# A chunked linear-attention and squared-ReLU kernel: how w and u are spread, how U and Y of the first chunks are interleaved, and a new order of the opening

## The chip, the core and the metric

The kernel runs on one core of a Trainium2 chip. The core has a matrix engine (TensorE, "PE" in the profile; its weight loads are "PEld"), a vector engine (VectorE, "DVE"), a scalar engine (ScalarE, "ACT"), a general engine (GpSimd, "POOL") and a queue engine (SyncE, "SP"). Each runs its own instructions in order and waits for the others by semaphores. Matrix products write to PSUM, eight banks of 128 x 512 fp32; everything else lies in SBUF, 128 partitions. The metric is device time in microseconds, the median of several runs; smaller is better.

## The reference

For each batch b (4) and head h (8), with 768 time steps and head size 48, a state of 48 x 48 is carried along:

```python
for t in range(S):
    cur = u[:, :, None] * k_t * v_t          # outer product over (d, e)
    y[:, :, t] = r_t @ (state + cur)
    state = w[..., None] * state + k_t * v_t
```

Here `w` and `u` have one value for each head and position, 8 x 48. The outputs of all heads form x, 3072 x 384, and the second half is a feed-forward layer: `(max(x @ w_in, 0) ** 2) @ w_out` with 2048 hidden columns, the result in fp32.

## The kernel before

**Tiling.** Time is cut into 24 units of 128 steps: six chunks for each of four batches. In a unit, all heads lie beside each other. The recurrence is done in closed form in a unit: k is multiplied by a decay factor `Wk` (rows w to a power that depends on the step) and r by `Wt`; both are transposed; their products give 128 x 128 scores for each head, masked by a triangle (`Bm`); Y is the scores times v plus r times the carried state `S0W`; U is k times v, which updates the state, scaled by `WLm`. The diagonal term is `dv` = v times the row sum of r x k x u (steps `P0`, `P1`, `du`, `dv`).

**Pairs.** The first four units (`PAIRED = 4`) are two pairs, two chunks of one batch each, loaded by one transfer per tensor (`lp`): partition p holds steps 2p and 2p + 1 of the 256. So the first chunk of a pair lies on partitions 0 to 63 and the second on 64 to 127. Half a in the names below is the even or odd step, half x (or s) the chunk. Products for a chunk of a pair therefore work on 64 rows of TensorE: U of a pair's chunk is eight products of 64 rows (L463), Y is two products with the identity that put dv in place (L428), four with the state for a second chunk (L436) and sixteen with the masked scores (L440).

**Factors.** `w` (L257) brings w as one row. `lw` (L266) takes its logarithm, `bw` (L269) multiplies a column of ones with that row and so spreads it over 128 partitions in a bank, and four Exp steps with a scale for each partition (L294, L298) make the factors of the pairs. `bc` (L303) puts the logarithm into columns, from which `WLcol` and `WLm` (L314) come. `u` is spread in the same way (`bu`, L272) and copied to SBUF (`ub`). `tab` loads ScalarE's tables ahead of that.

**Feed-forward.** `X` transposes a unit's outputs on TensorE (L489), `xTc` copies them; `xX` does both by a transposing transfer. `F1` (L505) multiplies with w_in, `re` and `sq` are ReLU and square, `F2` (L533) and `Fh` (L547) multiply with w_out; `os` and `out` copy and store. w_in comes in four pieces (`V`, L331) and w_out in four (`W`, L334) by transfers that GpSimd issues; SP issues the loads of r, k and v (`lp`, L325, `ld`, L321). `Z` (L565) multiplies the identity with itself into a bank that nobody reads: an empty product.

**Order.** The order of everything is written out by hand in `ORDER`. A step reads `name.unit...:engine/slots`, where the engine is A (ScalarE), D (VectorE), G (GpSimd), P (TensorE) or S (SP), and the slots say which bank or buffer the result takes. Each engine runs its own steps in this order. `Z.8:P/0` is two products of 512 columns, `Z.2` two of 128, `Z.7` one of 512 and three of 128. A `T` step transposes k and r of one unit past the pairs (L398), `TK` and `TR` those of a pair (L364), `KC` and `RC` copy them out of the bank, `Ap` and `Bp` are a pair's scores and masks (L384, L392).

Of the kernel before, what the change touches and what calls it, by code (L numbers as in the profile page):

```python
# [32 lines left out]
P1.3:G Bp.1.0.1:D/4 F1.0.0:P/6 re.0.3:D/0 dv.2:G F1.1.3:P/5 Wt.2:A re.0.0:A/1 W.1:G Bp.1.1.1:D/5 du.3:D/3 ld.v.5:S/5  # L33
Bp.1.0.0:D/6 Wk.2:A F1.1.0:P/4 F1.1.1:P/6 dv.3:G re.1.0:A/2 F1.0.1:P/0 rh.5:G/4 re.1.3:A/3 Bp.1.1.0:D/7 Y.3:P/4
sq.1.3:A/0 re.0.1:A/4 W.2:G kh.4:D/5 re.1.1:A/5 sq.1.0:D/1 Y.2:P/5 ld.k.6:S/6 xs.3:D/2 W.3:G F1.0.2:P/0 xs.2:A/3
rh.4:D/5 sq.0.0:A/2 X.3:P/6 W.0:G X.2:P/4 re.0.2:D/3 F1.1.2:P/5 xTc.3:A/0 sq.0.3:A/3 xTc.2:D/0 re.1.2:A/2 P0.4:D/4
T.4:P/0 Tc.4:D/4 F1.2.4:P/6 F1.2.7:P/4 sq.1.2:D/4 F1.2.5:P/5 re.2.4:D/1 re.2.7:A/0 ld.r.6:S/6 sq.0.2:A/5 F1.2.1:P/0
re.2.5:D/2 re.2.1:A/3 sq.2.5:D/6 sq.0.1:D/7 F1.2.0:P/6 kh.5:D/4 F1.2.2:P/4 sq.2.1:A/8 F1.2.6:P/5 re.2.2:A/2 re.2.0:D/4
T.5:P/0 re.2.6:D/3 F2.0.2:P/4 F1.2.3:P/6 ld.r.7:S/7 Tc.5:A/5 P1.4:D du.4:D/4 sq.1.1:D/9 A.4:P/5/0 sq.2.6:A/10
re.2.3:A/5 sq.2.3:A/11 F2.0.1:P/4 sq.2.0:A/12 F2.0.3:P/4 vb.4:G/4 Bm.4.1:D/0 Bm.4.0:D/1 sq.2.7:A/13 P0.5:D/1 A.5:P/6/0  # L40
Bm.5.1:D/2 sq.2.4:A/14 F2.1.1:P/5 Bm.5.0:D/3 F2.1.2:P/5 ld.k.7:S/7 dv.4:G Y.4:P/0 P1.5:G du.5:D/0 F2.3.2:P/6
sq.2.2:A/15 ld.v.7:S/6 ld.k.9:S/0 xs.4:D/4 F2.0.0:P/4 vb.5:A/5 Y.5:P/0 dv.5:D xs.5:D/0 F2.3.0:P/6 P0.6:G/0 P1.6:G
ld.v.6:S/7 F2.3.1:P/6 os.0:D/0 ld.r.9:S/0 X.4:P/0 xTc.4:D/1 U.4:P/4 F2.1.0:P/5 X.5:P/0 F2.1.3:P/5 S0.4:D xTc.5:D/1
rh.7:G/6 F1.3.0:P/4 os.1:D/1 F1.3.4:P/0 P0.7:G/2 re.3.0:D/3 out.1:S F1.3.2:P/5 kh.7:D/6 re.3.4:A/5 kh.6:G/0 F1.3.6:P/4
# [24 lines left out]
re.6.6:D/2 dv.13:G F2.9.0:P/0 XB.14:S/0 sq.6.6:A/15 du.12:D/3 A.13:P/2/1 sq.6.5:A/8 A.12:P/5/7 re.6.1:D/5 F2.8.1:P/4
sq.6.7:A/12 XB.15:S/6 Bm.12.0:D/2 P0.17:G/1 sq.6.2:A/16 F2.8.3:P/4 Bm.12.1:D/3 re.6.3:A/4 F2.8.0:P/4 ld.v.14:S/7  # L70
# [54 lines left out]
def kernel(  # L125
# [106 lines left out]
    for t in rk:  # L232
        nc.vector.memset(t[:, :, :, D:DP], 0.0)
# [403 lines left out]
```

## Time and profile before

| | us |
|---|---|
| median of three runs | 170.84 (170.64 to 170.85) |
| profiled execution, whole time | 171.19 |
| its span, first to last instruction | 169.5 |
| TensorE busy | 164.2 |
| VectorE busy | 137.1 |
| ScalarE busy | 101.9 |
| GpSimd busy | 99.9 |

The times below are microseconds from the start of the span. A group line names the line of the kernel, the engine, the operation, what it writes and reads, and how many there are. An engine's busy time counts matrix products as pipelined, so that products that overlap are one stretch; the end of a matrix product is modelled.

### The profile page before, as it was taken

The page shows a single profiled execution, that of the slowest core. Times are in us where ns is not written, and L with a number is a line of the kernel's source. Part 1 is how long each engine was busy: PE and PEld are TensorE (multiplying, and loading weights), DVE is VectorE, ACT ScalarE, POOL GpSimd, SP SyncE. Part 2 cuts the span into 40 slices and gives each one's busy share as a digit, 9 for nine tenths or more (in the row PEclk, how much of TensorE's full clock was granted, in tenths as well). Part 3 has the DMA queues.
Part 4 walks back from the last instruction along what each step waited for, and adds up shares of the span by engine and source line. Part 5 has one row for each costly group of instructions (what it writes and reads, how often), then busy time and mean ns, then how long its engine had stood idle before and what let it go on. Part 6 is the DMA issues. An engine that isn't in the chain of part 4 may idle for free.

```text
span 169.5 us, 4602 instructions
## 1 busy us (share of the span) xinstructions
PE 164.2 (97%) x1828; PEld 125.4 (74%) x1828; DVE 137.1 (81%) x255; ACT 101.9 (60%) x190; POOL 99.9 (59%) x122
## 2 busy tenths in 40 slices
PE   4999999999999999999999999999999999999993
PEld 1686989767866786888766888766888676898762
DVE  5669989997899999979999999998779975955300
ACT  4684686870685779249892359952099393254731
POOL 6799681277199608996699979399627550200000
PEclk9999999999999999999999999999999999999999
DMA  5999999991899798999997999965959672230032
GB/s 136 323 237 193 215 215 208 201 200 39 165 200 211 138 191 173 209 201 134 209 203 151 212 228 220 177 136 141 184 98 202 170 88 70 90 99 0 6 139 93
DMA packets 96137, 27.56 MB, mean 163 GB/s; under 512 B 90642, under 2 KB 96020, under 8 KB 96116
## 3 DMA queue, kind: packets, MB, share of 16 engines
q1 hardware_dynamic: 92416, 22.55, 66.4%
q0 software_dynamic: 2816, 3.54, 11.5%
q10 hardware_dynamic: 884, 1.18, 2.2%
q8 instruction: 14, 0.23, 0.6%
q14 instruction: 7, 0.06, 0.1%
HBM read 20.45 MB, written 4.72 MB: 149 GB/s over the span
## 4 chain that ended last, share of the span: by engine, by line
PE 95%; ACT 1%; DVE 1%; issue 1%; ACTq 0%
PE bank L505 37%; PE bank L533 36%; PE bank L411 3%; PE bank L463 2%; PE bank L452 2%; PE bank L364 2%; PE bank L489 2%; PE bank L450 2%; PE bank L547 2%; PE bank L440 1%; PE bank L269 1%; DVE Bm L392 1%; PE bank L303 1%; PE bank L272 1%; PE bank L398 1%; PE bank L428 1%
## 5 line engine op out<-in xcount | busy, mean ns | idle before, releaser
L505 PE MATMUL bank<-xT,W 128*128 128x256 bf16 (+1 forms) x672 | 70.0, 257 | 0.0
L533 PE MATMUL bank<-W,hq 128*128 128x384 bf16 x368 | 68.9, 326 | 0.0
L505 PEld LDWEIGHTS <-W 128*128 128x128 bf16 x672 | 56.9, 98 | 7.7
L515 ACT ACTIVATE hr<-bank 128x512 bf16<-128x512 f32 x67 | 38.7, 594 | 36.4 <-PE bank L505 27.8
L533 PEld LDWEIGHTS <-hq 128*128 128x128 bf16 x368 | 33.8, 98 | 18.2
L522 ACT ACTIVATE hq<-hr 128x512 bf16<-128x512 bf16 x70 | 41.0, 626 | 3.4 <-DVE hr L517 2.8
L419 DVE TENSOR_TENSOR Bm<-bank,maskJT 128x512 bf16<-128x512 f32 x40 | 25.7, 682 | 2.7 <-PE bank L411 2.7
L355 POOL TENSOR_TENSOR dv<-ldv,du 128x384 f32<-128x384 f32 (+1 forms) x18 | 15.9, 891 | 16.2 <-DVE du L350 11.3
L517 DVE TENSOR_SCALAR hr<-bank 128x512 bf16<-128x512 f32 x29 | 19.7, 686 | 6.6 <-PE bank L505 4.5
L347 POOL TENSOR_TENSOR P<-P,ub 128x384 f32<-128x384 f32 x15 | 16.0, 1070 | 13.1 <-DVE P L343 12.7
L340 POOL TENSOR_TENSOR rk<-ldr,Wt 128x384 bf16<-128x384 f32 x15 | 16.4, 1101 | 0.0
L343 POOL TENSOR_TENSOR P<-ldr,ldk 128x384 f32<-128x384 f32 x13 | 13.3, 1023 | 1.5 <-DMA ldk<-in_k_dram 1.2
L524 DVE TENSOR_TENSOR hq<-hr 128x512 bf16<-128x512 bf16 x26 | 12.4, 490 | 2.0 <-ACT hr L515 1.8
L484 POOL TENSOR_TENSOR S0W<-ts,WLm 128x384 bf16<-128x384 f32 x10 | 10.9, 1091 | 4.4 <-DVE ts L481 3.6
L475 DVE TENSOR_TENSOR xs<-bank,dv 128x384 bf16<-128x384 f32 x20 | 11.1, 553 | 3.0 <-PE bank L452 1.1
L337 POOL TENSOR_TENSOR rk<-ldk,Wk 128x384 bf16<-128x384 f32 x12 | 12.3, 1032 | 1.4 <-DMA ldk<-in_k_dram 1.4
L350 DVE TENSOR_REDUCE du<-P 128x8 f32<-128x384 f32 x24 | 12.9, 542 | 0.0
L253 DVE COPY os<-bank 128x384 f32<-128x384 f32 x11 | 6.1, 551 | 6.9 <-PE bank L533 6.9
L481 DVE TENSOR_TENSOR ts<-bank,S0W 128x384 f32<-128x384 f32 x16 | 8.7, 550 | 1.2 <-POOL S0W L484 0.8
L452 PE MATMUL bank<-vb,Bm 128*128 128x48 bf16 x160 | 9.5, 183 | 0.0
L251 ACT COPY os<-bank 128x384 f32<-128x384 f32 (+2 forms) x14 | 6.3, 458 | 4.5 <-PE bank L533 2.5
L452 PEld LDWEIGHTS <-Bm 128*128 128x128 bf16 x160 | 8.2, 96 | 1.0
(79 smaller groups left out, 177.8 us busy)
## 6 DMA issues: line engine op xcount, KB each, us to landing
ldr<-in_r_dram SPq DMA_DIRECT2D x20, 192.0 KB, 4.0
ldk<-in_k_dram SPq DMA_DIRECT2D x20, 192.0 KB, 4.2
ldv<-in_v_dram SPq DMA_DIRECT2D x20, 192.0 KB, 3.6
out_dram<-os SPq DMA_DIRECT2D x12, 192.0 KB, 2.1
W<-in_moe_w_in_dram POOLq DMA_DIRECT2D x4, 384.0 KB, 8.6
W<-in_moe_w_out_dram POOLq DMA_DIRECT2D x4, 384.0 KB, 6.4
out_dram<-os ACTq DMA_DIRECT2D x5, 192.0 KB, 3.5
ldr<-in_r_dram SPq DMA_DIRECT2D x2, 384.0 KB, 4.1
```

The lines of the kernel that those rows point to most:

```text
L340: e.tensor_mul(rk[slot[f"rk{i}"]][:, 0, :, 0:D], loaded("r", i), Do.factor("t", i % 2 if i < PAIRED else 2))
L343: e.tensor_mul(P0b[slot[f"P{i}"]], loaded("r", i), loaded("k", i))
L347: e.tensor_mul(t, t, bank("bu")[:, 0 : H * D].rearrange("p (h d) -> p h d", h=H) if i in EARLY_U else ub)
L350: e.tensor_reduce(dub[slot[f"dv{i}"]], P0b[slot[f"P{i}"]], axis=mybir.AxisListType.X, op=ALU.add)
L355: e.tensor_mul(dv_of(i) if i < PAIRED else dvb[slot[f"dv{i}"]], loaded("v", i), t)
L419: e.tensor_mul(Bmb[slot[f"Bm{i}{h}"]], heads(bank(f"bA{i}{h}"), 128), mask_b)
L452: e.matmul(y[:, hc, D * h : D * (h + 1)], m[h][:, hc, :], vb[:, 2 * hc + h, :], start=(c == 0), stop=True, skip_group_check=True,)
L505: e.matmul(hp[:, fi, :], W1[f // 4][:, c, 256 * (f // 2 % 2) : 256 * (f // 2 % 2 + 1)].rearrange("p (m j) -> p j m", j=2)[:, f % 2, :], xt ...
L515: e.activation(hr, hp, AF.Relu)
L517: e.tensor_scalar_max(hr, hp, 0.0)
L522: e.activation(hq, hr, AF.Square)
L533: e.matmul(bank(f"bO{i}")[:, 0:d_model], hqb[slot[f"hq{g},{f // m}"]][:, at : at + L], W2[q][:, f % 4, :], start=(seen[i] == 1 and f % 4 = ...
```

## The change

1. w and u are loaded as two rows of 192 values, on partitions 0 and 64. `bw` and `bu` become two products each, one on each row group, into two banks. The logarithm is taken after the spreading, on 128 partitions, half by half (`lw.0`, `lw.1`), into a tile `LW` in SBUF, and the Exp steps read that tile. `ub` is two copies.
2. For the pairs, `U.0` and `U.1` become `UP.0`, and `U.2` and `U.3` `UP.1`: the same sixteen products, taken from the two chunks in turn. Y becomes `YD` (dv and score products of both chunks in turn) and `YI` (the product with the carried state, for the second chunk, at the end of the sum instead of ahead of the scores).
3. The empty products are five single ones of 512 columns (`Z.4`).
4. The zero fills of `WLm` and of three of the seven rk buffers and the small step `nj` are steps of the order now (`mW`, `mR`, `nj`), on VectorE as before.
5. The order of the opening is new, the second chunks' r and k (`lp.r.1`, `lp.k.1`) are loaded first, the w_in pieces are issued later, T.4 and T.5 come ahead of the first `F1`, and some steps change engine (P0, P1, dv, vb, re, sq, xTc, os). `X.4` and `xTc.4` become `xX.4`. From Y.7 on, TensorE's steps are the same in the same order, with other banks.

```diff
-w:A mP.0:G mP.1:G lp.r.0:S/0 lp.k.0:S/0 tab:A lw:A Z.8:P/0 bw:P/0 lp.r.1:S/1 lp.v.0:S/0 mJ:G u:A lp.k.1:S/1 Wt.1:A/1
-lp.v.1:S/1 bc:P/2 P0.1:G/0 Wk.0:A/3 rh.1:D/0 ld.r.5:S/4 Wt.0:A/4 bu:P/5 kh.0:D/1 V.3:G WLcol:A P0.0:D/1 Wk.1:A/6
-rh.0:D/1 TR.0:P/7 ld.k.4:S/4 V.0:G rh.3:D/2 ub:A V.1:G rh.2:D/3 vb.0:A/0 vb.1:A/1 ld.r.4:S/5 kh.1:D/0 P1.0:G RC.0:A/0
-TR.1:P/2 kh.2:D/3 kh.3:D/2 TK.0:P/1 KC.0:A/1 V.2:G P1.1:D U.1:P/5 Z.2:P/4 TK.1:P/4 ld.k.5:S/5 du.0:D/0 dv.0:G RC.1:A/2
-du.1:D/1 dv.1:G Ap.0.1:P/7/3 Bp.0.1.1:D/0 vb.3:A/2 U.0:P/6 Ap.0.0:P/1/2 Bp.0.1.0:D/1 Bp.0.0.1:D/2 WLm:G KC.1:A/3
-Z.7:P/3 Ap.1.0:P/3/7 vb.2:A/3 U.3:P/2 Bp.0.0.0:D/3 P0.2:G/2 U.2:P/4 S0.0:D Y.0:P/1 ld.v.4:S/4 S0.2:D P1.2:G Y.1:P/6
-xs.0:A/0 ts.3:D/0 ts.1:D/1 X.0:P/4 Ap.1.1:P/1/2 xTc.0:D/0 du.2:D/2 xs.1:A/1 X.1:P/5 F1.0.3:P/4 xTc.1:A/1 P0.3:G/3
...
+mW:D w:A tab:A u:A Z.4:P/0 bw:P/1/2 Z.4:P/3 mR:D lw.0:A nj:D lw.1:A bc:P/4 Wt.1:A/5 lp.r.1:S/1 rh.3:D/3 lp.k.1:S/1
+Wk.1:A/6 kh.3:D/3 Wk.0:A/7 Wt.0:A/0 mP.0:G mP.1:G P0.2:G/0 kh.2:D/2 WLcol:A lp.k.0:S/0 rh.2:D/2 bu:P/1/3 TR.1:P/2
+kh.1:D/1 kh.0:D/0 TK.0:P/4 lp.r.0:S/0 ub.1:A Wt.2:A rh.0:D/0 rh.1:D/1 RC.1:A/0 ub.0:A P0.1:D/1 P1.1:D TR.0:P/6 P1.2:D
+P0.3:G/2 P1.3:D mJ:G WLm:G TK.1:P/3 Z.4:P/7 P0.0:G/3 KC.0:A/1 du.1:D/0 P1.0:G du.0:D/1 RC.0:A/2 Ap.0.1:P/0/5
+lp.v.0:S/0 vb.1:A/0 Bp.0.1.1:D/0 ld.k.4:S/4 Z.4:P/2 KC.1:A/3 V.1:G lp.v.1:S/1 V.2:G vb.0:A/1 ld.r.5:S/4 Ap.0.0:P/1/4
+ld.r.4:S/5 vb.2:A/2 Ap.1.1:P/6/7 vb.3:A/3 Z.4:P/2 Bp.0.1.0:D/1 Bp.0.0.0:D/2 Wk.2:A dv.0:G UP.0:P/5/3 Bp.0.0.1:D/3
+S0.0:D dv.1:G Ap.1.0:P/0/2 YD.0:P/1/4 Bp.1.0.1:D/4 rh.4:G/4 Bp.1.1.1:D/5 xs.0:A/0 kh.4:D/4 YI.1:P xs.1:A/1 UP.1:P/5/2
+ld.k.5:S/5 X.0:P/1 xTc.0:A/0 V.3:G kh.5:D/5 Bp.1.0.0:D/6 X.1:P/7 S0.2:D du.3:D/2 rh.5:G/5 T.4:P/4 T.5:P/1 xTc.1:A/1
+F1.1.1:P/7 V.0:G Tc.4:A/4 Tc.5:A/5 F1.0.1:P/0 F1.0.2:P/5 F1.1.2:P/4 re.1.1:A/0 re.0.2:A/1 dv.3:G Bp.1.1.0:D/7 du.2:D/3
+dv.2:D ts.1:D/0 ts.3:D/1 YD.1:P/6/1 A.5:P/7/5 Bm.5.0:D/0 re.1.2:A/2 sq.1.2:A/0 A.4:P/3/2 YI.3:P Bm.4.1:D/1 P0.5:G/4
+P1.5:G F1.0.3:P/4 xs.2:A/2 xs.3:A/3 P0.4:G/1 W.2:G X.2:P/6 X.3:P/7 xTc.3:D/0 xTc.2:A/0 F1.1.3:P/1 P1.4:D du.4:D/4
+re.0.3:A/3 F1.2.6:P/2 re.2.6:A/4 Bm.4.0:D/2 du.5:D/0 re.1.3:A/5 Bm.5.1:D/3 F1.1.0:P/6 re.1.0:A/2 sq.1.0:A/1 sq.0.3:A/2
...
         def w(e):
-            e.dma_start(out=wrow, in_=w.rearrange("h d -> (h d)").rearrange("(a n) -> a n", a=1))
+            Do.halves(e, wsrc, w)
+        def halves(e, t, row):
+            e.dma_start(
+                out=t.rearrange("(a q) n -> a q n", a=2)[:, 0, :],
+                in_=row.rearrange("h d -> (h d)").rearrange("(a n) -> a n", a=2),
+            )
+        def spread(e, t, to):
+            for h in range(2):
+                at = slice(64 * h, 64 * h + 1)
+                e.matmul(
+                    bank(f"{to}{h}")[:, 0 : H * D // 2], ones[at], t[at], start=True, stop=True, skip_group_check=True,
+                )
...
-        def lw(e):
-            e.activation(lrow[:, :, 0:D], wrow.rearrange("a (h d) -> a h d", h=H), AF.Ln)
-        def bw(e):
-            e.matmul(bank("bW")[:, 0 : H * D], ones, lrow[:, :, 0:D], start=True, stop=True)
+        def lw(e, h):
+            e.activation(LW[:, HP * h : HP * (h + 1), 0:D], Do.spread_half("bW", h), AF.Ln)
+        def spreading(e, o, scale):
+            e.activation(o, LW[:, :, 0:D], AF.Exp, scale=scale)
...
+        def YD(e, q):
+            y = [heads(bank(f"bY{2 * q + x}"), 2 * D) for x in range(2)]
+            for a in range(2):
+                for x in range(2):
+                    e.matmul(
+                        y[x][Do.half(a)], identity[Do.half(x), Do.half(x)],
+                        dv_of(2 * q + a)[Do.half(x)].rearrange("p (a e) d -> p a (e d)", e=2),
+                        start=True, stop=False, skip_group_check=True,
+                    )
+            for hc in range(HP):
+                for h in range(2):
+                    for a in range(2):
+                        for x in range(2):
+                            e.matmul(
+                                y[x][:, hc, D * h : D * (h + 1)],
+                                Bmb[slot[f"Bm{q}{a}{h}"]][Do.half(x), hc, :],
+                                vbb[slot[f"vb{2 * q + a}"]][Do.half(x), 2 * hc + h, :],
+                                start=False, stop=True, skip_group_check=True,
+                            )
+        def YI(e, i):
...
+        def UP(e, q):
+            o = [heads(bank(f"bU{2 * q + x}"), 2 * D) for x in range(2)]
+            for hc in range(HP):
+                for a in range(2):
+                    for x in range(2):
+                        e.matmul(
+                            o[x][:, hc, :],
+                            pair(rk[slot[f"rk{2 * q + a}"]], 1, hc)[Do.half(x)],
+                            vbb[slot[f"vb{2 * q + a}"]][Do.half(x), 2 * hc : 2 * hc + 2, :].rearrange("p a b -> p (a b)"),
+                            start=(a == 0), stop=(a == 1), skip_group_check=True,
+                        )
```

More of the change, by code (lines that the diff above doesn't have):

```diff
@@ L19 @@
 PAIRED = 4
-EARLY_U = ()
 COLS = (slice(0, 288), slice(288, 384))
 GROUPS = [1, 1, 2, 2, 2, 2, 2, 2, 2, 2, 2, 2, 1, 1]
-POOLS = dict(ldr=8, ldk=8, ldv=8, ws=3, rk=7, P=5, dv=5, vb=8, rkT=7, bank=8, Bm=8, xs=5, xT1=2, xT2=3, hr=6, hq=28,
-    os=8, ts=2)
+POOLS = dict(ldr=8, ldk=8, ldv=8, rk=7, P=5, dv=5, vb=8, rkT=7, Bm=8, xs=5, xT1=2, xT2=3, hr=6, hq=28, os=8, ts=2, bank=8)
 ORDER = """
-w:A mP.0:G mP.1:G lp.r.0:S/0 lp.k.0:S/0 tab:A lw:A Z.8:P/0 bw:P/0 lp.r.1:S/1 lp.v.0:S/0 mJ:G u:A lp.k.1:S/1 Wt.1:A/1
@@ L112 @@
+outh.23.1:S
 """
@@ L303, in bc @@
                 e.matmul(
-                    bank("bc")[:, hc : hc + 1], pair(lrow.rearrange("p (o a) b -> p o a b", o=1), 0, hc), ones[:, 0:1],
+                    bank("bc")[:, hc : hc + 1], pair(LW[0:1].rearrange("p (o a) b -> p o a b", o=1), 0, hc), ones[0:1, 0:1],
                     start=True, stop=True, skip_group_check=True,
```

251 lines of the change are left out of this document (118 added, 133 removed).

## The prediction

> **What bounds the kernel now.** I read the page first, then the chain of waits, then the timeline of the first 26 us, then the transfers in stretches of two us.
>
> ```profile
> span 169.5 us, 4602 instructions
> ...
> PEclk9999999999999999999999999999999999999999
> ...
> PE 95%; ACT 1%; DVE 1%; issue 1%; ACTq 0%
> ```
>
> 95% of the chain that ended last is TensorE's own. Its products pass at full pace once they begin (row 18.29 below: 72 products of 128 columns in 4.02 us, 56 ns each), and the change leaves their number alone; from Y.7, the second output of the fourth pair, its steps are the same ones in the same order. So time can only go where TensorE waits or works slowly. The chain shows where:
>
> ```profile
> 2.67 0.53 ACT lrow L266
> 3.24 1.64 PE bank L269 x2
> 4.88 1.50 PE bank L303 x8
> 6.38 1.49 PE bank L272 x2
> 7.87 2.67 PE bank L364 x24
> ...
> 11.62 0.83 PE bank L364 x8
> 12.45 0.38 PE bank L384 x16
> ...
> 12.85 0.82 DVE Bm L392 x2
> ...
> 15.49 0.28 PE bank L428 x2
> 15.77 0.50 PE bank L440 x16
> ...
> 16.56 0.28 PE bank L436 x4
> ...
> 18.29 4.02 PE bank L505 x72
> ...
> 25.93 0.46 PE bank L398 x8
> ```
>
> Columns: start, length, engine, line. The logarithm of w (2.67) is spread over the partitions (3.24), column sums of it follow (4.88), u is spread (6.38), then come 32 transposes, the score products L384, their masking on VectorE, Y (from 15.49), and the first dense W products at 18.29. Everything ahead of 18.29 is a chain of latencies through TensorE, ScalarE and VectorE; behind it TensorE is full. The change must be priced by how much earlier TensorE has the same work behind it.
>
> The rows of the timeline that give durations (start, length, engine, line, operation, how many):
>
> ```profile
> 2.94 0.38 DVE L234 MEMSET WLm<- 128x384 f32 x1
> ...
> 4.92 0.56 ACT L298 ACTIVATE bank<-bank,tcol 128x384 f32<-128x384 f32 x1 [1.73 <-PE bank L269]
> ...
> 6.94 1.47 DVE L340 TENSOR_TENSOR rk<-ldr,bank 128x384 bf16<-128x384 f32 x3
> 9.11 1.01 ACT L251 COPY rkT<-bank 128x1024 bf16<-128x1024 bf16 x1
> 10.48 0.82 PE L463 MATMUL bank<-vb,rk 64*128 64x96 bf16 x8
> ...
> 12.38 0.42 PE L384 MATMUL bank<-rkT,rkT 48*64 48x128 bf16 x16
> ...
> 12.73 0.51 PE L463 MATMUL bank<-vb,rk 64*128 64x96 bf16 x8
> 12.75 0.74 POOL L314 COPY WLm<-wcol 48x192 f32<-48x192 f32 x2
> 12.85 2.49 DVE L392 TENSOR_TENSOR Bm<-bank,maskP 128x512 bf16<-128x512 f32 x4 [1.30 <-PE bank L384]
> ...
> 14.79 0.70 PE L463 MATMUL bank<-vb,rk 64*128 64x96 bf16 x16 [0.19 <-DVE Bm L392]
> ...
> 30.81 0.61 PE L398 MATMUL bank<-identity,rk 128*128 128x128 bf16 x8
> ```
>
> **Part 1, the spread of w and u.** Before: the logarithm of one row waits for the table, then two instructions of 384 columns take 1.64 us, and the first Exp (row 4.92) starts at 4.92. After: the raw row is spread first, as two halves of 192 columns on row groups 0 and 64, and the logarithm follows on 128 partitions. w had landed by 2.67; one empty product (half of what two took from 1.97 to 3.00) ends at 2.5, and the spread starts there. Bounds: 1.64 if the halves follow each other, 0.9 if they run at once; it ends at 3.4 to 4.1. The two logarithms of 192 columns cost between 0.28 (half of row 4.92) and 0.56 each, the first partly under the second product. The first Exp then starts at 4.0 to 4.9; I take 4.45, 0.5 ahead. VectorE's four products with the factors follow it from 5.0, 0.49 each (row 6.94, three in 1.47), and end at 7.0. TensorE has the column sums (1.5) and u (0.9 to 1.64) from 4.45 on: free at 6.9 to 7.6. The transposes begin at 7.3 instead of 7.87.
>
> **Part 2, transposes, scores, masks.** Eight U products (0.82) and two empty ones leave the midst of the transposes; 32 of them at the 0.104 to 0.11 us of rows 7.87 and 11.62 make 3.4, with one empty product 11.1. ScalarE's four copies (1.01 each, row 9.11) bind instead: TR.1 is done at 8.2, three copies and half a copy of u later the scores start at 11.6, against 12.38 now. VectorE meanwhile has the last two factors' products to 9.0, then six steps of half a us (P0.1, P1.1, P1.2, P1.3, du.1, du.0) to 12.1 and four masks, 2.49, to 14.6; now these end at 15.34. YD.0 starts at 14.8, Y.0 does at 15.49. Vector and scalar work that stood behind other engines now stands in front of the masks: that is why 0.8 shrinks to 0.7.
>
> GpSimd must have dv.0 and dv.1 ready by then:
>
> ```profile
> 5.61 0.99 POOL L343 TENSOR_TENSOR P<-ldr,ldk 128x384 f32<-128x384 f32 x1 [1.24 <-DMA ldk<-in_k_dram]
> 6.55 2.50 POOL L331 DMA_DIRECT2D W<-in_moe_w_in_dram  x3
> ...
> 11.18 1.61 POOL L355 TENSOR_TENSOR dv<-ldv,du 128x384 bf16<-128x384 f32 x2 [0.37 <-DVE du L350]
> ```
>
> From 5.6 on (its first operand is loaded as early as now): two P0 (2.0), the mask J (0.5), WLm (0.74, row 12.75), P0.0 and P1.0 (2.0) to 10.85; V.1 and V.2 issued (0.83 each, row 6.55) to 12.5; dv.0 and dv.1 (1.61) to 14.1. In time. rh.4 to 15.1, V.3 to 15.9, rh.5 to 16.9, V.0 to 17.7. All four V are issued 4 to 9 us later than now; part 5 prices that.
>
> **Part 3, interleaved U and Y.** Do products on the two row halves overlap?
>
> ```profile
> 32.66 0.40 PE L411 MATMUL bank<-rkT 48*128 48x128 bf16 x8
> ```
>
> L411 alternates row halves: eight products of 128 columns take 0.40 where eight full-height transposes of 128 columns, 57 ns apart on the chain (row 25.93), take 0.61. That is 0.21 less in seven steps: some 27 ns apart. L463 today does not alternate: 44 ns (row 14.79, sixteen in 0.70). So the pair's U should fall from 0.70 to 0.40, the dv products from 0.56 (two rows like 15.49) to between 0.28 and 0.56, and the 32 products of 48 columns from 1.00 (two rows like 15.77) to between 0.42 and 1.00. I take 0.28 and 0.72: YD is 1.0 for a pair where the same work now takes 1.56.
> The Trainium skill, "TensorE: Matmul & The Clock Gate", section "Wait — 56ns, not 53.3ns?", speaks against this: starts never come closer than about 25 ns, however small the product. By it 32 products cost at least 0.80, YD 1.08 at least, and the two pairs lose 0.16 together. The trace differs from the rule: the sixteen products of L384 on four quadrants take 0.42 in all, 17 ns apart when the 0.15 that a group stands beyond its chain (0.61 against 0.46) is taken off.
>
> **Part 4, up to the first dense products.** From 14.8: YD.0 1.0, YI.1 0.28 (row 16.56), UP.1 0.40 to 0.70, X.0 and X.1 0.6, T.4 and T.5 0.92 (row 25.93 twice): 3.3 us, F1 at 18.1 (17.4 to 18.9 by the bounds). F1 starts at 18.29 now, but T.4 and T.5 are then still to be done; with them the same state is reached at 19.2. Lead: 1.1, between 0.3 and 1.8. The second pair then costs 1.28 for YD.1 and YI.3 where Y.3 and Y.2 cost 1.84: 0.55 more, 0 to 0.9. Part of it is lost: ScalarE now has the copies Tc.4 and Tc.5 (1.01 each), three ReLU of 0.6, a square and xs.2 and xs.3 between 17.9 and about 23.3, and X.3 sits on TensorE's queue behind xs.3. TensorE gets there at 23.4 after five F1 groups, YD.1, A.5, A.4 and YI.3, and waits up to 0.5. I charge 0.4.
>
> **Part 5, the loads.** Whatever binds the loads must still deliver.
>
> ```profile
> 1.94 1.12 SPq L325 DMA_DIRECT2D ldr<-in_r_dram  x1
> 3.10 1.15 SPq L325 DMA_DIRECT2D ldv<-in_v_dram  x1
> ...
> ldr<-in_r_dram SPq DMA_DIRECT2D x1, 384.0 KB, 4.7
> ...
> ldv<-in_v_dram SPq DMA_DIRECT2D x1, 384.0 KB, 4.8
> ...
> q1 hardware_dynamic: 1707, 0.64, 116.8%
> ...
> q0 software_dynamic: 313, 0.32, 93.4%
> q1 hardware_dynamic: 350, 0.07, 28.9%
> ...
> W<-in_moe_w_in_dram POOLq DMA_DIRECT2D x1, 384.0 KB, 6.0
> ...
> W<-in_moe_w_in_dram POOLq DMA_DIRECT2D x1, 384.0 KB, 10.6
> ```
>
> The last column is the time from issue to landing; the q rows are packets in 6 to 8 us (q1 alone) and in 12 to 14 us (both). Third and fourth load land at 6.6 and 7.9; they are now k.0 and r.0, wanted at 7.0 and 8.0. A load of 1024 packets takes 1.2 us while SP's queue is alone (1707 in 2 us), 5.9 beside GpSimd's weights (350 in 2 us). The four V land 6.0 after the first issue (6.55) and then every 2.7 us (the last, issued at 10.0, at 20.6), so their packets start 3.3 us after an issue. After: V.1 issued at 10.85 lands at 16.9, V.2 at 19.5, V.3 at 22.2, V.0 at 24.9. TensorE wants them at 18.1, 19.4, 22.7 and 25.2: covered, with 0.3 to 0.5 to spare where now several us are. The tenth load, ld.k.5, would land at 7.9 + 6 x 1.2 = 15.1 alone; V.1's packets start at 14.15, and what is still to come moves five times slower: 810 packets at worst, 4.6 us, 18.8. I take the middle, 17.0. VectorE reaches kh.5 at 14.6 + 0.5 (S0.0) + 1.25 (two masks) + 0.5 (kh.4) = 16.85, so it hardly waits. That load is the thinnest spot.
>
> VectorE's fills and njcol are the same set in another order and end about where today's last one does (row 2.94: 3.32). Its next step waits for the first Exp at 4.45 or later; without that cover a fill moved ahead would cost its length, 0.38 for WLm. Behind Y.7 only banks and buffers are renumbered and a few output issues change queue or place; I cost that at nothing, because TensorE's full queue hides it. X.4 leaves TensorE for a transposing transfer on SP: 0.17 less (three products of 57 ns).
>
> **Sum.** 1.1 + 0.55 - 0.4 + 0.17 = 1.42 us less, made against the profiled execution's own 171.19 us (span 169.5 and 1.7 around it): 169.77. That execution lay 0.35 over the median of the runs, 170.84, so the forecast is 169.4. By the bounds of the parts: 0.3 + 0 - 0.5 + 0.17 to 1.8 + 0.9 + 0.17, that is 170.9 to 168.0.
>
> **Rivals.**
> (a) ld.k.5 lands late, at 18.8 or after. kh.5 is in the midst of VectorE's queue: behind it stand the masks of the second pair, S0.2, du.3, du.2, dv.2; T.5 waits for it on TensorE, and all F1 behind T.5. F1 would start at 19.9, 1.8 late: 171.2, slower than before. It decides from a landing 1.4 late, at 18.4. For it: 350 against 1707 packets. Against: V.1 cannot be issued sooner, since P1.0 waits for the copy of u at about 9.6.
> (b) Half pace. Row 10.48's eight products take 0.82, row 12.73's, of the same shape, 0.51; transposes stand 111 ns apart in row 7.87 and 57 in row 25.93. The granted clock says 9 in every slice, so that column doesn't show it, but TensorE passed work at half pace until about 12.3, some 4.5 us after the transposes at 7.80 made it dense. After, the work from 11.1 to 14.8 is thin. If the full pace came only 4.5 us after YD.0, at 19.3, that stretch would lose half of 4.5: 171.7. Against: the 3.8 us of transposes are as dense as before. The Trainium skill, "TensorE: Matmul & The Clock Gate", section "Part 1: The HAM clock gate", describes such a gate, opened after about 3.4 us of sustained work, and its section "Part 4: PE-mode transpose" says that transposes don't count as such work: by the second, fewer empty products would make this rival likelier. The trace bears out a single change of pace, but here it came at the end of 4 us of transposes, against the second.
> (c) V.3 or V.0 a us late, GpSimd having 0.3 to 0.5 in hand: 170.4, at the edge of what can be told.
> (d) The row halves don't overlap, so the change doesn't do what it says there: UP loses its 0.3, YD 0.56, YD.1 part of the same: 170.4. Against it: L411 and L384.
> (e) The early transposes already run at full pace, since they come denser: 1.2 us more on TensorE, of which ScalarE's copies let through 0.6 at most: 168.8.
>
> **Chances.** The forecast 0.50, (a) 0.16, (b) 0.10, (c) 0.10, (d) 0.07, (e) 0.07. A change under 0.2% (0.34 us) can't be told from none: faster 0.65 (forecast, (e), half of (c) and (d)), same 0.09 (the other half), slower 0.26 ((a), (b)). The likeliest case's own range is 168.6 to 170.3. To hold 8 in 10 it must reach to (a), and leaves out the far end of (b) and the sum of all good bounds: 168.3 to 171.5.
>
> **What would show it.** First Exp at about 4.45, first transposes 7.3, scores 11.6, first YD products 14.8, T.5 at 17.6, F1 at 18.1; 16 U products in 0.40 and YD in 1.0; q1 at some 1700 packets in each two us up to 14. Wrong: VectorE idle ahead of kh.5 with the load as releaser, transposes at 111 ns or F1 products at 107 after 12.4, TensorE waiting at F1 for a W transfer, or a first Exp at 4.9 or later.

## The result, and the profile after

| | us | ratio to before, 95% interval |
|---|---|---|
| before, median | 170.74 (170.60 to 170.85) | |
| after, median | 178.3 (177.66 to 178.63) | 1.0439 [1.0407, 1.0471] |
| after, profiled execution | 177.66, span 175.9 | |

The change makes the kernel slower by 4.4%, some 7.5 us; forecast were 169.4 us and a range to 171.5. Some executions of these kernels took about 4 us longer; the ratios and medians below leave them out, and of the run with one-row loads, whose profile fell on such an execution, only the first rows are used.

The page of the kernel after, its span and its chain by engine:

```profile
span 175.9 us, 4591 instructions
...
PE 43%; DMA 19%; POOL 14%; SPq 10%; issue 5%; DVE 4%; ACT 3%; ACTq 0%; POOLq 0%; DVEq 0%
```

TensorE had 95% of the chain before. Now it has 43%, and transfers, GpSimd and SP's queue have as much together (19, 14 and 10): TensorE waits for them. Where it does is seen in the busy time by stretches (columns: stretch, its length, busy us of TensorE, its weight loads, VectorE, ScalarE and GpSimd, each with a count of instructions, then granted clock, DMA share, GB/s). One row for the kernel before:

```profile
28.00:64.00 36.00, 36.00 (x366) 26.47 (x364) 32.19 (x62) 23.34 (x43) 19.39 (x20) 1.00 0.87 170
```

The same stretch after, and the pieces of it that are not full:

```profile
28.00:64.00 36.00, 30.43 (x289) 21.71 (x287) 30.53 (x49) 16.45 (x32) 18.84 (x19) 1.00 0.76 144
```

```profile
32.00:36.00 4.00, 2.18 (x16) 1.18 (x15) 4.00 (x5) 0.24 (x1) 3.19 (x4) 1.00 1.15 203
36.00:40.00 4.00, 2.81 (x25) 2.13 (x26) 2.40 (x6) 2.01 (x4) 0.00 (x0) 1.00 0.48 85
...
52.00:56.00 4.00, 2.36 (x19) 1.72 (x18) 4.00 (x7) 3.94 (x8) 1.63 (x2) 1.00 1.09 215
```

Between 28 and 64 us TensorE idles 36.00 - 30.43 = 5.57 us, where it idled 0 before; the span grew by 6.4. In the stretch 32 to 36 VectorE is full with five instructions: one of them must be very long. Between 36 and 40 GpSimd does nothing at all.

How far behind is TensorE when the two orders meet again? A correction belongs here: the text ahead of the prediction, and the prediction, say that TensorE's steps are the same from Y.7 on. F2.0.0 stands behind Y.7 after and well ahead of it before; they are the same from X.6 on. X.6 is the first row with L489 below (before), and with L530 (after), from the two timelines:

```profile
54.99 0.33 PE L489 MATMUL bank<-identity,xs 128*128 128x128 bf16 x3
```

```profile
60.85 0.34 PE L530 MATMUL bank<-identity,xs 128*128 128x128 bf16 x3 [0.49 <-DVE xs L516]
```

By then 5.86 us are lost, of the 6.4 by which the span grew. The opening itself, from the timeline of the kernel after:

```profile
0.80 1.09 ACTq L254 DMA_DIRECT2D wsrc<-in_w_dram  x1
...
3.62 1.01 PE L268 MATMUL bank<-wsrc,ones 1*128 1x192 f32 x4 [1.03 <-DMA wsrc<-in_w_dram]
...
5.22 0.58 ACT L316 ACTIVATE bank<-LW,tcol 128x384 f32<-128x384 f32 x1
...
7.96 3.67 PE L388 MATMUL bank<-identity,rk 128*128 128x128 bf16 x32
...
10.43 2.33 DVE L371 TENSOR_TENSOR P<-P,ub 128x384 f32<-128x384 f32 x3
...
12.15 0.64 PE L408 MATMUL bank<-rkT,rkT 48*64 48x128 bf16 x16
...
13.60 2.47 DVE L416 TENSOR_TENSOR Bm<-bank,maskP 128x512 bf16<-128x512 f32 x4
...
14.34 0.51 PE L495 MATMUL bank<-vb,rk 64*128 64x96 bf16 x16
...
16.41 0.57 PE L461 MATMUL bank<-vb,Bm 64*128 64x48 bf16 x32
...
18.60 1.09 PE L422 MATMUL bank<-identity,rk 128*128 128x128 bf16 x16 [0.33 <-DVE rk L361]
...
19.53 1.50 PE L546 MATMUL bank<-xT,W 128*128 128x128 bf16 x24
...
21.34 1.51 PE L546 MATMUL bank<-xT,W 128*128 128x128 bf16 x24 [0.31 <-DMA W<-in_moe_w_in_dram]
```

The first Exp (L316) is at 5.22, forecast 4.45, before 4.92; the transposes at 7.96, forecast 7.3, before 7.87. The first dense W products (L546) start at 19.53 with T.4 and T.5 done; the same state was reached at 19.2 before, by the prediction's reckoning, and 18.1 was forecast. So the lead of 1.1 us isn't there, but against the kernel before the opening loses only 0.3 us.

Now the stretch with the holes. Rows of the timeline after from 30 to 55 us, in order of time, those of VectorE (DVE), GpSimd (POOL), SP's queue and TensorE that belong together:

```profile
30.67 1.33 SPq L537 DMA_TRANSPOSE xT<-xs  x1
31.12 1.04 POOL L361 TENSOR_TENSOR rk<-ldk,Wk 128x384 bf16<-128x384 f32 x1
31.75 2.59 DVE L565 TENSOR_TENSOR hq<-hr 128x512 bf16<-128x512 bf16 x1
33.99 1.20 POOL L364 TENSOR_TENSOR rk<-ldr,Wt 128x384 bf16<-128x384 f32 x1
34.27 0.68 DVE L558 TENSOR_SCALAR hr<-bank 128x512 bf16<-128x512 f32 x1
35.00 0.81 PE L574 MATMUL bank<-W,hq 128*128 128x384 bf16 x4 [1.70 <-DVE hr L558]
38.77 2.78 PE L546 MATMUL bank<-xT,W 128*128 128x256 bf16 x24 [1.19 <-DMA xT<-xs]
40.92 2.65 SPq L428 DMA_TRANSPOSE rkT<-rk  x2
43.62 0.57 SPq L345 DMA_DIRECT2D ldk<-in_k_dram  x1
46.93 0.99 POOL L361 TENSOR_TENSOR rk<-ldk,Wk 128x384 bf16<-128x384 f32 x1 [11.74 <-DMA ldk<-in_k_dram]
50.63 0.88 DVE L364 TENSOR_TENSOR rk<-ldr,Wt 128x384 bf16<-128x384 f32 x1
51.43 1.35 DVE L367 TENSOR_TENSOR P<-ldr,ldk 128x384 f32<-128x384 f32 x1
54.31 0.54 DVE L519 TENSOR_TENSOR S0W<-bank,WLm 128x384 bf16<-128x384 f32 x1
54.90 0.82 PE L546 MATMUL bank<-xT,W 128*128 128x256 bf16 x6 [1.64 <-DVE S0W L519]
```

Three stories stand in these rows.

- **A square that is held.** sq.2.5 on VectorE (31.75) takes 2.59 us. While it lasts GpSimd runs four products back to back, from 31.12 to 35.19. Behind the square on VectorE stands re.2.1 (34.27), and F2.2.2 on TensorE waits 1.70 us for it. All squares on VectorE in a view by line (minimum, median, maximum in ns), before and after:

```profile
L524 DVE TENSOR_TENSOR hq<-hr x26: 411/418/925, 23.0 to 158.8; 128x512 bf16<-128x512 bf16 x26
```

```profile
L565 DVE TENSOR_TENSOR hq<-hr x29: 406/420/2587, 29.1 to 165.3; 128x512 bf16<-128x512 bf16 x29
```

- **A transfer that is late.** xX.4 is issued at 30.67, and F1.3.2 waits for it until 38.77. In the transfers of 32 to 34 us, the packets of GpSimd's queue (q0, the last three w_out pieces) fill the engines, and none of SP's queue (q1) moves:

```profile
q0 software_dynamic: 277, 0.40, 113.2%
...
xT<-xs SPq DMA_TRANSPOSE x1, 8.0
```

- **Loads behind a waiting instruction.** rh.6 on VectorE stands behind re.3.2, which waits for F1.3.2. SP waits for rh.6 with XB.6 (40.92), and the load of k for unit 9 stands behind XB.6 and XB.7 (43.62). GpSimd's next step needs that load and starts at 46.93, after 11.74 idle us. Its work then runs beside VectorE's, whose two-operand steps stretch (0.88 and 1.35 for what takes 0.55 elsewhere), S0.5 is reached at 54.31, and F1.3.5 waits 1.64 us for the bank that S0.5 reads.

### The profile page after: what moved, and what is told of

It reads as the page before. It is cut to its first block, busy times and chain, and to the rows that moved or that the text cites. A ratio compares the mean times of both kernels' runs of the same rounds, so it can differ in the third digit from the quotient of the medians.

```text
span 175.9 us, 4591 instructions
## 1 busy us (share of the span) xinstructions
PE 162.6 (92%) x1826; PEld 123.4 (70%) x1826; DVE 141.3 (80%) x255; ACT 101.8 (58%) x193; POOL 99.6 (57%) x121
## 4 chain that ended last, share of the span: by engine, by line
PE 43%; DMA 19%; POOL 14%; SPq 10%; issue 5%; DVE 4%; ACT 3%; ACTq 0%; POOLq 0%; DVEq 0%
PE bank L546 19%; PE bank L574 17%; SPq L345 6%; DMA ldk<-in_k_dram 5%; DMA W<-in_moe_w_in_dram 5%; DMA xT<-xs 5%; POOL rk L361 4%; POOL P L367 3%; SPq L428 3%; POOL rk L364 3%; DMA ldr<-in_r_dram 2%; POOL P L371 2%; DMA wsrc<-in_w_dram 2%; PE bank L435 2%; PE bank L588 2%
## 5 line engine op out<-in xcount | busy, mean ns | idle before, releaser
L546 PE MATMUL bank<-xT,W 128*128 128x256 bf16 (+1 forms) x672 | 70.5, 257 | 3.7 <-DVE S0W L519 1.6
L546 PEld LDWEIGHTS <-W 128*128 128x128 bf16 x672 | 56.8, 98 | 12.1 <-issue 2.7
L563 ACT ACTIVATE hq<-hr 128x512 bf16<-128x512 bf16 x67 | 39.5, 627 | 4.7 <-DVE hr L558 4.2
L361 POOL TENSOR_TENSOR rk<-ldk,Wk 128x384 bf16<-128x384 f32 x14 | 14.6, 1050 | 13.8 <-DMA ldk<-in_k_dram 13.8
L379 POOL TENSOR_TENSOR dv<-ldv,du 128x384 f32<-128x384 f32 (+1 forms) x16 | 13.8, 874 | 12.6 <-DVE du L374 12.6
L371 POOL TENSOR_TENSOR P<-P,ub 128x384 f32<-128x384 f32 x13 | 13.7, 1060 | 12.2 <-DVE P L367 11.4
L565 DVE TENSOR_TENSOR hq<-hr 128x512 bf16<-128x512 bf16 x29 | 17.3, 606 | 2.9 <-ACT hr L556 2.7
L364 POOL TENSOR_TENSOR rk<-ldr,Wt 128x384 bf16<-128x384 f32 x15 | 17.4, 1162 | 0.0
L367 POOL TENSOR_TENSOR P<-ldr,ldk 128x384 f32<-128x384 f32 x14 | 14.6, 1042 | 2.1 <-DMA ldk<-in_k_dram 1.9
L248 ACT COPY xT<-bank 128x384 bf16<-128x384 bf16 x10 | 4.6, 480 | 15.2 <-PE bank L530 10.3
L248 ACT COPY os<-bank 128x384 f32<-128x384 f32 (+2 forms) x17 | 7.8, 463 | 4.5 <-PE bank L574 2.5
L250 DVE COPY os<-bank 128x384 f32<-128x384 f32 x8 | 4.4, 551 | 5.7 <-PE bank L574 5.7
```

The source lines that it names most:

```text
L361: e.tensor_mul(rk[slot[f"rk{i}"]][:, 1, :, 0:D], loaded("k", i), Do.factor("k", i % 2 if i < PAIRED else 2))
L364: e.tensor_mul(rk[slot[f"rk{i}"]][:, 0, :, 0:D], loaded("r", i), Do.factor("t", i % 2 if i < PAIRED else 2))
L367: e.tensor_mul(P0b[slot[f"P{i}"]], loaded("r", i), loaded("k", i))
L371: e.tensor_mul(t, t, ub)
L379: e.tensor_mul(dv_of(i) if i < PAIRED else dvb[slot[f"dv{i}"]], loaded("v", i), t)
L546: e.matmul(hp[:, fi, :], W1[f // 4][:, c, 256 * (f // 2 % 2) : 256 * (f // 2 % 2 + 1)].rearrange("p (m j) -> p j m", j=2)[:, f % 2, :], xt ...
```

## The experiments

Times are medians; in the diffs a step's name stands as in the order, and "..." is what lies between.

**One wait at a time.** First the late transfer: X.4 back on TensorE with a copy by ScalarE.

```diff
-X.5:P/4 re.0.1:A/5 xTc.5:A/1 ... xX.4:S/1
+X.4:P/3 X.5:P/4 xTc.4:A/1 re.0.1:A/5 xTc.5:A/1
```

> The changed kernel with X.4 back on TensorE and its copy xTc.4 on ScalarE, instead of the transposing transfer. Theory T (the transfer waits behind three w_out pieces, TensorE's F1.3 waits for it, and SyncE's queue slips with everything behind F1.3): 172.5 to 174.5 us, no TensorE idle stretch over 1 us between 32 and 40. Theory V (VectorE's square sq.2.2 is held by GpSimd for 2.6 us, and that is what starts the slip): 176.5 to 178. Theory O (the loss was made before 31 us, in the opening): 177.5 to 178.5.

Measured: 179.59 us, 1.0475 [1.0415, 1.0535], over the ranges of all three theories: not faster than the change itself. The waits of TensorE from 28 to 62 us (line, releaser, us in total, times, longest):

```profile
PE bank L546 <- DVE S0W L519: 1.6, 1, 1.6
PE bank L574 <- DVE hr L558: 1.1, 1, 1.1
PE bank L574 <- ACT hr L556: 0.9, 1, 0.9
```

The 1.19 us for xT are gone, but ScalarE, with one copy more ahead of re.0.1, now makes TensorE wait 0.9 instead. Then the square: first sq.2.2 to ScalarE, with the transfer as it is and with X.4 on TensorE.

```diff
-sq.2.2:D/14
+sq.2.2:A/14
```

> The changed kernel with the one square sq.2.2 on ScalarE, which was idle then, instead of VectorE; the transfer stays. Theory T: 177 to 178.5, since F1.3 still waits for the transfer until about 38.7. Theory V: 174 to 176. Theory O: 177.5 to 178.5.

> Both edits. Theory T: as with X.4 alone or up to 1 us less. Theory V: as with the square alone or little less, 174 to 176. If the two waits lie in line, each hiding the other: clearly less than either alone, 171 to 173. Theory O: 177.5 to 178.5.

Measured: 178.58 us, 1.0453 [1.0425, 1.0481], and 179.19, 1.0477 [1.043, 1.0524]. The first lies 0.1 over the range that theories T and O share, the second shows no gain over X.4 alone, and theory V, for which the square was moved, misses in both. But neither touches the square that is held: the step just ahead of re.2.1 in VectorE's order is sq.2.5, not sq.2.2. So the right square by itself:

```diff
-sq.2.5:D/6
+sq.2.5:A/6
```

> The changed kernel with the square sq.2.5, the one that VectorE held for 2.6 us from 31.75, on ScalarE. Theory L (VectorE is held while GpSimd runs four products back to back; that and the transfer of X.4 lie in line, each hiding what the other costs): 177 to 178.5, since F1.3 still waits for the transfer until 38.6, but F2.2.2 starts 1.5 us or more earlier than 35.0. Theory Q (SyncE's queue: XB.6 and the loads behind it come late for a reason of their own): 177 to 178.5 as well, with XB.6 still issued at 40.9.

Measured: 179.43 us, 1.0497 [1.0467, 1.0527], 0.9 over both ranges. Its waits in the same stretch:

```profile
PE bank L546 <- DMA xT<-xs: 3.5, 1, 3.5
PE bank L546 <- DVE S0W L519: 1.5, 1, 1.5
```

This is the instructive row. The wait for re.2.1 is gone, and the wait for xT has grown from 1.19 to 3.54: TensorE arrives 1.56 us earlier (36.02 against 37.58) at a transfer that is there no earlier (it was issued at 31.27 against 30.67, and the products that need it start at 39.56 against 38.77). The two waits, 1.70 and 1.19, cover the same stretch of time, so the later one takes up what the earlier one gives back.

**Both.** sq.2.5 on ScalarE and X.4 on TensorE, its copy behind re.0.1:

```diff
-sq.2.5:D/6 ... X.5:P/4 re.0.1:A/5 xTc.5:A/1 ... xX.4:S/1
+sq.2.5:A/6 ... X.4:P/3 X.5:P/4 re.0.1:A/5 xTc.4:A/1 xTc.5:A/1
```

> The same with X.4 on TensorE too, its copy on ScalarE behind the ReLU re.0.1. Theory L: F1.3 starts at 35.5 to 36.5, XB.6 is issued by 38.5, and the time is 173 to 175.5. Theory Q: 177 or more, XB.6 at 40.5 or later.

Measured: 175.79 us, 1.0295 [1.0261, 1.0329], 2.5 us under the change and 0.3 over theory L's range. TensorE is full from 24 to 48 us, but then waits for S0.5:

```profile
PE bank L546 <- DVE S0W L519: 2.3, 1, 2.3
```

One thing differs besides: the copy xTc.4 stands behind re.0.1 here and stood ahead of it in the run of X.4 alone, where TensorE waited 0.9 us for re.0.1. X.4 alone with the copy in the better place wasn't run, so it isn't shown that undoing the transfer alone gains nothing.

Is the transfer bad in itself? The kernel before with only this edit:

```diff
-X.4:P/0 xTc.4:D/1 U.4:P/4
+xX.4:S/1 U.4:P/4
```

> The kernel before with X.4 as a transposing transfer, all else as it was. Theory T says that the transfer costs because of what it is queued behind; the w_out pieces of the kernel before have landed by 33 us and X.4 comes at 39, so: 170.3 to 171.5. If a transposing transfer in that place costs by itself: 172 or more.

Measured: 171.33 us, 1.0037 [0.9993, 1.0081], no difference that can be told. The transfers of 28 to 40 us in that kernel, with the time from issue to landing last:

```profile
xT<-xs SPq DMA_TRANSPOSE x1, 3.3
```

So its kind costs nothing there. That its place behind the w_out pieces is what costs is read from the packets: from 36 to 40 us, while this transfer is under way, none of GpSimd's queue moves.

**The third wait.** S0.5 moved ahead of four steps that it doesn't need, on top of the former run:

```diff
-os.3:D/0 rh.9:D/1 P0.9:D/3 ... P1.9:D S0.5:D T.9:P/0
+os.3:D/0 S0.5:D rh.9:D/1 P0.9:D/3 ... P1.9:D T.9:P/0
```

> The changed kernel with sq.2.5 on ScalarE and X.4 on TensorE (175.8 us), and S0.5 besides moved on VectorE to stand right behind os.3, ahead of rh.9, P0.9, a square and P1.9; the instructions are the same. Theory (waits in line, S0.5 the third of them): S0.5 runs at about 47.7 instead of 51.5, the 2.28 us that F1.3.5 waited for it go, TensorE's 48 to 52 is full, and the time is 173.5 to 174.1 us. Rival (VectorE and GpSimd share a fixed amount of work between 44 and 56 us, and TensorE stalls for it wherever S0.5 stands): the stall turns up at the next step, 175.3 to 176.1 us.

Measured: 175.48 us, 1.0298 [1.0249, 1.0347]: nothing gained, the theory fell and its rival held. TensorE's waits from 28 to 70 us:

```profile
PE bank L422 <- DVE rk L364: 1.4, 1, 1.4
PE bank L530 <- DVE xs L516: 0.9, 1, 0.9
```

The stall went to T.9, whose operand rh.9 now comes later. So the cause was looked for further back, where GpSimd is idle: at the loads behind XB.6.

**SP's queue.** The loads of unit 9 ahead of XB.6 and XB.7; in a second kernel also r of units 8 and 11:

```diff
-XB.6:S/6 ... XB.7:S/1 ld.k.9:S/2 ... ld.r.9:S/2 ... ld.r.8:S/3 ld.r.11:S/1
+ld.k.9:S/2 ld.r.9:S/2 XB.6:S/6 ... XB.7:S/1 ... ld.r.8:S/3 ld.r.11:S/1
```

> The run with sq.2.5, X.4 and S0.5 put back (175.5 us), and on SP's queue ld.k.9 and ld.r.9 besides stand ahead of XB.6 and XB.7 instead of behind them; nothing else. Theory (the root of the second stall is SP's queue: XB.6 waits for rh.6 until 38.3 us, the loads behind it land at 44.5, GpSimd is idle from 35.8 until then and afterwards works beside VectorE, whose steps it stretches from 0.42 to 0.55 to 1.26 to 1.37): ld.k.9 is issued at about 28 to 29, GpSimd runs kh.9, P0.7 and P1.7 from 35.8 to 38.8, and of the three stretched steps between 46.5 and 51.2 (2.4 us too long together) about half is gone, 174.0 to 175.0 us. Rival (VectorE meets GpSimd wherever its work is put, and the stall only moves to 36 to 40): 175.2 us or more.

> As the run beside it, with ld.r.8 and ld.r.11 also ahead of XB.6. Theory (the loads behind XB.6 hold GpSimd): rh.8 and rh.11 run by 42 us too, rh.9 and P0.9 on VectorE take 0.55 each instead of 1.37 and 1.35, the wait for rh.9 (1.4 us) goes, and the time is 173.0 to 174.2 us. Rival (the stall only moves): 175.2 us or more.

Measured: 173.47 us, 1.0140 [1.0098, 1.0183], and 173.77, 1.0168 [1.0133, 1.0202]. The first is under the time that the theory gave, the second in its range; two more loads bring nothing more. Without any arithmetic changed or moved, 2 us are gone. The timeline of the first of them shows both the gain and what is left:

```profile
34.48 3.12 DVE L565 TENSOR_TENSOR hq<-hr 128x512 bf16<-128x512 bf16 x1
...
49.05 0.55 DVE L364 TENSOR_TENSOR rk<-ldr,Wt 128x384 bf16<-128x384 f32 x1
49.52 0.55 DVE L367 TENSOR_TENSOR P<-ldr,ldk 128x384 f32<-128x384 f32 x1
```

rh.9 and P0.9 are back at 0.55 each. But GpSimd now goes on without a break from 31.4 to 38.5, and another square is held beside it, 3.12 us long; TensorE waits 0.9 us for the step behind it. The rival (the stall only moves) is right by that much. In the second kernel GpSimd pauses at 35.8, that square takes 1.21 and TensorE's 0.9 us are not there, but the time is no better. Both runs hold the move of S0.5 too; the loads without it, beside sq.2.5 and X.4, weren't run. Last, the loads alone in the kernel after:

> The changed kernel as it is, with ld.k.9 and ld.r.9 ahead of XB.6 and XB.7 on SP's queue and nothing else changed. Theory (three causes that lie in line: the held square, X.4's late transfer, SP's queue): the first two waits (1.70 us for re.2.1 and 1.19 us for xT) stay, only the stall at 50 to 56 us shrinks, 176.3 to 178.0 us. Rival (SP's queue is the root of all of it): 175 us or less.

Measured: 176.51 us, 1.0318 [1.0293, 1.0344], as the theory gave it. Its waits:

```profile
PE bank L546 <- DMA xT<-xs: 1.6, 1, 1.6
PE bank L574 <- DVE hr L558: 1.3, 1, 1.3
```

The wait for S0.5 is gone, the first two stay. So several causes lie in line, and SP's queue is one of them, not the root of all.

**The parts by themselves.** The interleaved U and Y in the kernel before, with its own order:

```diff
-P1.1:D U.1:P/5 Z.2:P/4 ... U.0:P/6 ... U.3:P/2 ... U.2:P/4 S0.0:D Y.0:P/1 ... Y.1:P/6
+P1.1:D Z.2:P/4 ... UP.0:P/6/5 ... UP.1:P/4/2 S0.0:D YD.0:P/1/6 ... YI.1:P
...
-Y.3:P/4 ... Y.2:P/5
+YD.1:P/5/4 YI.3:P
```

> The kernel before, its order kept, with U and Y of both chunks of a pair interleaved (UP, YD, YI at the places of U.0, U.2, Y.0, Y.1, Y.3). Row halves overlap in the changed kernel's trace (thirty-two Y products in 0.51 us), so: 169.6 to 170.6, 0.1 to 0.7% faster. If waiting for both chunks takes the gain back: 170.7 to 171.3.

Measured: 169.86 us, 0.9941 [0.992, 0.9962]. This beats both kernels. Its chain (start, length, engine, line, count):

```profile
17.77 4.02 PE bank L549 x72
...
22.08 0.51 PE bank L437 x32
```

32 score products of the second pair in 0.51 us, where sixteen took 0.50 before (row 15.77 of the prediction's chain), and F1 at 17.77 against 18.29.

Then the spread of w and u in the kernel before, with the fills as steps at the head of the order. In the first run u was requested behind the logarithm, in the second right behind the tables, in the third w and u are loaded as one row each, and both products of a spread work on one row group (the order below is that of the second and third):

```diff
-w:A ... tab:A lw:A Z.8:P/0 bw:P/0 ... u:A ... bu:P/5 ... ub:A
+w:A ... tab:A u:A Z.4:P/0 Z.4:P/0 bw:P/0/1 lw.0:A lw.1:A ... bu:P/5/0 ... ub.0:A ub.1:A
```

> The kernel before, its order kept, with the spread of w and u alone (two rows, two row halves, logarithm after it; two empty products ahead of it as before). The trace of the changed kernel had w land at 3.48 and the first Exp at 5.22, against 4.92 before: 170.8 to 171.6, up to 0.5% slower. If the spread is what the forecast took it for: 169.8 to 170.5. If it costs the whole opening: 172 or more.

> The kernel before, its order and its U and Y, with the spread of w and u alone, u requested right behind the tables (it stood behind the logarithm in the run of the spread alone, 172.8 us). Theory (the transfer of two rows lands w about 1.1 us later, and that is more than the halves gain): first Exp at 5.3 to 5.6 against 4.92, u spread before VectorE needs the transposes' operands, time 171.0 to 171.5 us. Rival (the prediction's part 1, that the spread gains half a us, and the loss in the former run was the late u alone): 170.2 to 170.6 us.

> As the spread alone with u early, but w and u are loaded as one row of 384 values each and both products of a spread take their halves from that row, on one row group. Theory (the shape of the transfer is what is late): w lands at about 2.7 instead of 3.7, the two products follow each other in 1.6 instead of 1.0, first Exp at 4.8 to 5.0, and the time is 0.3 to 0.7 us under the spread with two rows. Rival (w lands late in any case, because the queue or the other loads hold it): the same landing as with two rows, a spread 0.6 longer, and a time 0.3 to 0.7 us over it.

Measured: 172.84 us, 1.0112 [1.0085, 1.0139]; 171.75, 1.0061 [1.0037, 1.0085]; 171.93, 1.0055 [1.0034, 1.0075]. The first lies where the whole opening was to be at fault, and about 1 us of it goes when u is requested early; the second is 0.25 over its theory's range and far from its rival's. Rows of the second:

```profile
3.69 1.01 PE L267 MATMUL bank<-wsrc,ones 1*128 1x192 f32 x4 [0.67 <-DMA wsrc<-in_w_dram]
...
5.28 0.59 ACT L315 ACTIVATE bank<-LW,tcol 128x384 f32<-128x384 f32 x1
```

and of the third:

```profile
0.81 0.53 ACTq L253 DMA_DIRECT2D wsrc<-in_w_dram  x1
...
2.95 1.64 PE L266 MATMUL bank<-wsrc,ones 1*128 1x192 f32 x4
...
4.99 0.58 ACT L314 ACTIVATE bank<-LW,tcol 128x384 f32<-128x384 f32 x1
```

With two rows the halves overlap (1.01 us instead of 1.64) and start 0.74 later; with one row it is the other way round. First Exp 5.28 and 4.99, before 4.92: neither form is ahead. The theory was right about the landing and wrong about the time: the third kernel is no faster than the second, the difference of the ratios is 0.0006 with intervals of 0.002 either way. In the profiled execution of the second, its 0.6% are not lost in the opening. X.6 starts at 54.88, 0.11 ahead of the kernel before, and a row of 18 products at 145.04 is level with it (145.02). Then 30 products start at 148.66 instead of 148.01, after a wait of 0.47 for a transposing transfer (xT) that is issued at 144.82, as before (144.80), and takes 3.8 us to land, where it took 2.3 before and TensorE didn't wait. These 0.65 us are the whole difference of the two profiled spans (170.1 and 169.5). Why that transfer lands later isn't shown.

Both parts together, still in the order of before:

> The kernel before with its order, the spread of w and u (u early) and the interleaved U and Y: parts one and two of the change without part five. Theory (the parts add up and the loss is in the order): 169.9 (interleave alone) plus what the spread alone costs in the run beside it, 170.2 to 170.7 us, so the new order alone costs 7 to 8 us. Rival (the parts need the new order, or each other's slots, and lose without it): 172 us or more.

Measured: 171.14 us, 1.0018 [1.0002, 1.0034], half a us over the theory's range but within the intervals of the parts' sum (0.9941 and 1.0061 give 1.0002). Its trace has X.6 at 54.23, 0.76 ahead of the kernel before, and loses that in a wait of 0.96 for the same late transfer, at 148.24. The same two parts with the new order, which takes in the moves between engines, other empty products, and X.4 by transfer, make 1.0439. So the new order costs 4.2%, about 7.2 us, and it is the whole loss.

| kernel | us | ratio |
|---|---|---|
| change | 178.3 | 1.0439 |
| change, loads of unit 9 ahead | 176.51 | 1.0318 |
| change, sq.2.5 and X.4 back | 175.79 | 1.0295 |
| the same, S0.5 ahead | 175.48 | 1.0298 |
| the same, S0.5 and the loads of unit 9 ahead | 173.47 | 1.0140 |
| before with spread and interleave | 171.14 | 1.0018 |
| before with interleave alone | 169.86 | 0.9941 |

## Why the prediction was wrong, step by step

**The step that failed** is the sum's scope, in the first paragraph and part 5: "So time can only go where TensorE waits or works slowly", and then terms for the opening, up to the second pair at 23.4, and for X.4, and none for the 30 us up to Y.7, whose order is new on every engine. Of what lies behind Y.7 the prediction says "I cost that at nothing, because TensorE's full queue hides it", and it silently took the same for the stretch ahead of it. That argues in a circle: the queue was full because the other engines delivered in time, and their order is what was rewritten. In its place the runs showed 5.57 us of waits between 28 and 64 us, mostly from three causes in line: sq.2.5 and X.4 (2.5 us together, no gain from either alone as run), and the loads of unit 9 (about 2.0 us on top of these, 1.8 by themselves: 178.3 less 176.51). Some 2.3 us of the order's cost remain between 173.47 and 171.14. The busy times of these two kernels' traces say where. Up to X.6 TensorE is busy for 50.4 us in both, but X.6 starts at 56.88 instead of 54.23. TensorE idles 1.3 us more in the first 28 us (5.1 against 3.9) and 1.3 us behind that, 0.86 of it for the step behind the held square. So the new opening costs too: up to 28 us TensorE idles 0.7 to 1.4 us more in the three traces looked at (the kernel after, and the two with loads moved) than the old order does with the same two parts. Against the kernel before that hardly shows, because the interleaving gains there (with it alone X.6 is at 53.79, 1.2 ahead).

**X.4** was credited with 0.17 us, three products less. It brought a wait of 1.19 us. The prediction counted what leaves TensorE and not what the transfer queues behind, though it had a row for just that: 350 packets against 1707 beside GpSimd's pieces.

**Part 1** was right that the halves overlap (1.01, in its bounds of 0.9 to 1.64) and wrong that w lands as before: a transfer of two rows takes 1.09 us to issue instead of 0.53, and its spread starts at 3.62 where 2.5 was forecast. The lead of 0.5 became a lag of 0.3. In the kernel before, that lag didn't last: the part alone is 0.6% slower, but its trace loses this at 148 us.

**Part 2** forecast transposes and scores 0.66 and 0.55 us early, mostly the error of part 1 handed on, and the end of the masks 1.5 early (16.07, 14.6 forecast). Besides, three P1 steps on VectorE took 2.33 (row 10.43) where 1.5 was charged; a product of GpSimd ran beside them from 10.41 to 11.41.

**Part 3** held. The row halves overlap: 32 score products in 0.51 us on the chain (0.72 was taken, 0.42 to 1.00 the bounds), the four dv products of a pair in 0.29 (0.28 taken), its U in 0.51 (0.40 taken). At 16 ns each, the score products come closer than the 25 ns that the prediction weighed against its own reading. By itself the part gains 0.6%, 1.0 us; the prediction's own terms for it (0.30, 0.56 and 0.55) come to 1.41, of which it gave back 0.4.

**Part 4** gave a lead of 1.1 at F1; measured is a lag of 0.3. V.2 was late by 0.31, a small form of rival (c).

**The rivals.** (a) and (d) didn't come: the operand of T.4 and T.5 cost 0.33 us (row 18.60), the halves overlap. (b) didn't either: the 24 products at 19.53 take 1.50, 62 ns each. (e) asked for transposes at full pace: the 32 of them took 3.67, 115 ns each. All rivals lay in the opening, as did the sum but for X.4. That was the blind spot.

## What to carry to other kernels

Where an order is rewritten, walk each in-order queue over the whole stretch that changed, the DMA issues among them, and ask at every instruction that waits what stands behind it; a full bottleneck engine hides others only as long as they deliver on the old schedule. Undo suspected waits together as well as singly: where two are in line, each experiment alone can show no gain where the two together do. An idle stretch of an engine off the path (GpSimd, 36 to 47 us) is a lead to follow, because the work that it misses there returns later beside the engine that then binds.

## What the runs showed of the hardware

A VectorE product of two tiles in SBUF beside back-to-back GpSimd products took 2.59 us, and 3.12 in another run, instead of 0.42, while VectorE steps that read a bank kept their 0.54 to 0.68 us. How long depends on GpSimd's run of products: the square of 3.12 us began at 34.48, and GpSimd went on with products at 35.38 and 36.34; the same square in the kernel with two more loads moved began at 34.87, GpSimd paused at 35.80, and it took 1.21. The Trainium skill, "SBUF — State Buffer", section "Who interferes with whom", says that these two engines share a pair of ports as an exclusive lock, and that a VectorE instruction with two SBUF inputs contends with a GpSimd one that reads SBUF. The traces agree, and show more: the square issued at 31.75 outlasted not only the GpSimd instruction that was running (31.12) but those that followed at 32.09 and 33.04 as well. A square that began at 104.47, just ahead of a GpSimd product at 104.58, took 0.43, so not every square beside GpSimd is held.

The transposing transfer of X.4 took 8.0 us from issue to landing behind GpSimd's w_out pieces and 3.3 us in the kernel before, where none was under way. A transfer of two rows of 192 values took 1.09 us to issue, one row of 384 took 0.53.
